# Two score banks instead of one tile of two, five W2 splits on VectorE, and a drain list in thirds of an L1 piece, in a fused attention and mixture-of-experts kernel

## The chip, the cores and the metric

The kernel runs on one core of a Trainium2 chip. The metric is the device time of one execution in microseconds (us), the median over several runs. Engines are called PE (TensorE, matmul), DVE (VectorE), ACT (ScalarE), POOL (GpSimd) and SP (SyncE, which only issues transfers here).

## The reference

Chunked attention feeds a top-1 mixture of experts:

```python
scores = scale * np.matmul(q_c, k_c.transpose(0, 1, 2, 4, 3))     # 64 x 64 within each chunk
attn = softmax(scores); x = matmul(attn, v_c)                     # as 4608 tokens x 512
do_compute = (x @ w_skip) > 0
e_idx = np.argmax(xc @ w_gate, axis=1)                            # one of 8 experts, gate_w its probability
h = np.maximum(xc[mask] @ w1[e], 0.0)                             # 512 -> 1024
y[mask] = gate_w[mask, None] * (h @ w2[e])                        # 1024 -> 512
out[do_compute] = xc + y
```

## The kernel before, in words

**Attention loop (L677 to L716).** 36 tiles of 128 tokens pass through a software pipeline: scores (PE, L240), their copy to SBUF (ACT, L245), row maximum (DVE, L250), subtraction (POOL, L255), exp (ACT, L259), transposes (PE, L266; ACT copy L271), the product with V (PE, L279), normalisation (ACT L285, DVE L290 and L292), transposes of the result (PE, L307), its split into a high and a low float16 part (ACT L312, DVE L317), and the router's logits (PE, L324). Every float32 operand that goes through the float16 matmuls is held as such a pair, high (ACT) and low (DVE).

**Routing.** For each of four groups of tiles, `route` (L374) is a generator of small steps, most of them on DVE: expert choice, ranks (PE, L402 to L406), a one-hot table (L434 to L442), and its product on PE (L446), which is added to `acc` (L450). After the last group, `tables()` (L810) walks through the rest: `order()` sorts the experts by size (L543 to L560, and the order goes to SP as `sexp`, with which the weights of the later experts are loaded), `finish_idx`, `select()` (L564 to L574, whose `sidx` the POOL gathers need), and `plan()` (L581 to L617).

**First expert, early.** Expert 3 is worked on first, and its first 256 rows ("the first unit") are gathered before the attention ends. Its W1 is converted during the loop (L357, L358). Its W2 arrives as eight pieces of 128 rows, two to a staging buffer `wst` (four buffers in all). `w2_scales` (L360) lets ACT write each piece's high part and scale the piece in place; `w2_splits` (L367) lets POOL subtract the high part to get the low one (L369). L1 of the first unit is the generator `l1_steps` (L479): eight pieces, each 12 matmuls of 128x256 into one PSUM bank, in three steps of 4 matmuls, then ACT (L490) and DVE (L491) empty the bank into `ht`.

**The drain (L719 to L764)** is a list written by hand: the last two tiles' attention steps, the router's steps, and, between them, `take(l1, n)`, `take(scales, n)` and `take(splits, n)`, which pull n steps from the three generators. Each engine then runs its own instructions in the order in which this list issued them. While the attention pools are alive, L1's pieces use the two halves of the score tile `spq` in turn (`early_hp`, L651). `spq` is one tile of two PSUM banks, and the built program makes a matmul into either half wait for the readers of the other.

**After the drain** the attention's PSUM is given back, and L1 continues in three `hp` banks. The loop over units (L845) finishes the first unit's L1, then runs L1 of the second unit (128 rows, the third early block, 128 columns to a matmul), then L2 of the first unit in two phases (`l2_split`, L515: phase 0 uses W2's high parts, phase 1 the low parts; PE lines L518), two blocks into two `sp` banks. Behind these matmuls, `take(steps, 1)` issues one step of `tables()`, and `take(splits, 1)` one split. Then comes L2 of the second unit (L511), the third unit of expert 3 (80 rows), and the other seven experts, with `conv_chunk` (ACT L223, DVE L224) converting their weights.

Of the kernel before, what the change touches and what calls it, by code (L numbers as in the profile page):

```python
# [44 lines left out]
XT_AT = 4  # L45
# [64 lines left out]
def moe_attention_kernel(ctx: ExitStack, tc: tile.TileContext, qk: bass.AP, vv: bass.AP, cst: bass.AP, crow: bass.AP, wall: bass.AP, out: bass.AP):  # L110
# [73 lines left out]
    spq = ps_p.tile([P, 2, H, CH], F32, name="spq")  # L184
# [49 lines left out]
    def pe_scores(t):  # L234
        q = T[t].pop("q").rearrange("p (c j s) -> p c j s", c=2, j=KC)
        k = T[t].pop("k").rearrange("p a (c j s) -> p c j a s", c=2, j=KC)
        sp = spq[:, t % 2]
        for j in range(KC):
            for c in range(2):
                nc.tensor.matmul(sp[halves[c], 2 * j:2 * j + 2, :], q[:, c, j, :], k[:, c, j], start=True, stop=True, skip_group_check=True)  # L240
        T[t]["sp"] = sp
# [118 lines left out]
    def w2_scales():  # L360
        for st, hi, _ in cw2:
            nc.scalar.activation(hi, st, AF.Copy, scale=SW)
            yield
            nc.scalar.activation(st, st, AF.Copy, scale=SW)
            yield

    def w2_splits():  # L367
        for st, hi, lo in cw2:
            nc.gpsimd.tensor_tensor(lo, st, hi, op=ALU.subtract)  # L369
            yield  # L370
# [280 lines left out]
    def early_hp():  # L651
        hps[0] += 1
        return spq[:, (hps[0] + 1) % 2].rearrange("p h s -> p (h s)")
# [67 lines left out]
    take(l1, 1)  # L721
# [4 lines left out]
    take(scales, 1)  # L726
# [5 lines left out]
    take(l1, 3)  # L732
    ac_exp(b)
    take(scales, 1)
    take(splits, 1)
# [7 lines left out]
    take(l1, 1)  # L743
# [5 lines left out]
    take(splits, 1)  # L749
# [5 lines left out]
    take(l1, 2)  # L755
# [3 lines left out]
    take(scales, 2)  # L759
    take(splits, 1)  # L760
    pe_logits(a)
    take(l1, 3)
# [47 lines left out]
    def tables():  # L810
        for n in (3, 0, 0, 0, 0, 2, 1, 1, 0, 1, 0, 1, 0, 1) + (0,) * 9 + (1,):
            for _ in range(n):
                route_step()
            yield
        route_step()
        yield
# [28 lines left out]
    for i, (p, bs, offs, n) in enumerate(units):  # L845
# [16 lines left out]
        for done in l1:  # L862
            at += 1
            if not i:
                take(steps, 1)
                take(scales, 2)
# [9 lines left out]
        if not i:  # L876
            for _ in l1_steps(xt, lambda: w, hc, units[1][3], hp_of[0], lambda fc: None):
                take(steps, 1)
                take(scales, 2)
            ys = [ps_s.tile([P, H, CH], F32, name="sp").rearrange("p h s -> p (h s)") for _ in bs]  # L880
            for phase in range(2):
                for y, o in zip(ys, offs):
                    for _ in l2_split(y, ht, w, o, phase):
                        take(steps, 1)
                        take(splits, 1)
                        for m in range(XGB):
                            fetch(m)
            for b, y in zip(bs, ys):
                prev.append(blk_out([(y, 0, P)], recs_b[b], xgs[b]))
# [98 lines left out]
```

## Time and profile before

| what | value |
|---|---|
| median of 3 runs | 362.99 us (361.44 to 364.69) |
| the profiled execution | 363.88 us, of which 362.1 us are the span from first to last instruction |
| mean granted PE clock | 0.966 |

| stretch, us of the span | what runs | PE busy | granted PE clock | DMA share |
|---|---|---|---|---|
| 0 to 122 | attention loop | 111.23 | 1.00 | 0.95 |
| 122 to 158 | drain, L1 of the first two units | 28.23 of 36 | 0.81 | 0.39 |
| 158 to 182 | L2 of the first two units | 19.87 of 24 | 0.86 | 0.47 |
| 182 to 192.5 | third unit | 9.58 of 10.5 | 1.00 | 0.93 |
| 192.5 to 300 | experts 2 to 6 in the sorted order | 107.12 of 107.5 | 1.00 | 0.68 |
| 300 to 362.1 | the rest | 53.62 of 62.1 | 0.96 | 0.37 |

A row of a timeline gives the start, the duration, the engine, the line, the tile that is written and those that are read, the count, and in brackets how long the engine had been idle and what ended it. A waits row gives the waiting engine and line, what it waited for, the total, the times, and the longest.

### The profile page before, as it was taken

To read this page: it belongs to the slowest core of one execution; us is meant where nothing else is said; L and a number is where in the kernel's file an instruction comes from. 1 tells how busy PE (TensorE), PEld (TensorE's weight loads), DVE (VectorE), ACT (ScalarE), POOL (GpSimd) and SP (SyncE) were. 2 spreads that over 40 slices of the span, in tenths; PEclk is the share of its full clock that TensorE was granted. 3 is DMA by queue.
4 is the path that set the end of the run, shared out by engine and by line. 5 is a ranking of instruction groups with operands and counts; after the bars stand their busy time and mean duration, and the time that the engine had idled before them with its cause. 6 is when DMAs were issued, how large, how long until landed. Compare 5 with 4: busy or idle time off the path is not lost.

```text
span 362.1 us, 10135 instructions
## 1 busy us (share of the span) xinstructions
PE 329.6 (91%) x3996; PEld 234.3 (65%) x3996; DVE 259.0 (72%) x481; ACT 192.1 (53%) x368; POOL 115.9 (32%) x116
## 2 busy tenths in 40 slices
PE   4799899999989877985989999999999999999991
PEld 1588778888878755851465544765755757668580
DVE  5368798888889933789486995785867968767430
ACT  1488887777777746510354744453643644446120
POOL 7333233333335231038260055225127322111111
PEclk9999999999999985998799999999999999999997
DMA  6999999999999990045284677876567667564000
GB/s 215 328 320 302 333 334 310 307 338 323 329 312 326 365 361 17 3 135 140 95 311 172 223 246 259 276 234 212 186 224 233 216 216 232 186 196 146 31 23 29
DMA packets 34981, 81.85 MB, mean 226 GB/s; under 512 B 4831, under 2 KB 4832, under 8 KB 34930
## 3 DMA queue, kind: packets, MB, share of 16 engines
q1 hardware_dynamic: 31826, 71.83, 60.3%
q0 software_dynamic: 3104, 9.33, 7.2%
q8 instruction: 33, 0.54, 0.6%
q14 instruction: 18, 0.15, 0.1%
HBM read 67.11 MB, written 14.17 MB: 224 GB/s over the span
## 4 chain that ended last, share of the span: by engine, by line
PE 53%; DVE 10%; issue 2%; POOL 2%; ACT 2%; POOLq 0%; DVEq 0%; ACTq 0%
PE sp L511 24%; PE hp L486 19%; PE xt L475 2%; DVE ht L491 2%; DVE ys L530 2%; PE spq L486 1%; DVE wset L224 1%; POOL wset L369 1%; PE spq L240 1%; PE sp L518 1%; PE o L279 1%; PE xp L307 1%; DVE emp L459 1%; PE pt L266 1%; POOL xg L227 1%
## 5 line engine op out<-in xcount | busy, mean ns | idle before, releaser
L486 PEld LDWEIGHTS <-wset 128*128 128x128 f16 x960 | 80.8, 100 | 30.7 <-issue 13.2
L486 PE MATMUL hp<-xt,wset 128*128 128x288 f16 (+8 forms) x912 | 94.6, 264 | 3.4 <-DVE ht L491 3.2
L511 PE MATMUL sp<-wset,ht 128*128 128x512 f16 (+7 forms) x504 | 92.3, 381 | 0.0
L224 DVE SCALAR_TENSOR_TENSOR wset<-wst,wset 128x1024 f16<-128x1024 f32 x56 | 67.6, 1217 | 8.2 <-ACT wset L223 8.0
L511 PEld LDWEIGHTS <-ht 128*128 128x128 f16 (+7 forms) x504 | 41.2, 102 | 41.7 <-issue 3.4
L223 ACT ACTIVATE wset<-wst 128x1024 f16<-128x1024 f32 x56 | 57.9, 1049 | 2.9 <-DMA wst<-in_wall 2.9
L255 POOL TENSOR_TENSOR sc<-sc,mx 128x512 f32<-128x512 f32 x36 | 37.6, 1044 | 66.7 <-DVE mx L250 66.6
L490 ACT ACTIVATE ht<-hp 128x288 f16<-128x288 f32 (+8 forms) x76 | 27.5, 362 | 59.2 <-PE hp L486 57.9
L227 POOL DMA_INDIRECT out<-ys,sidx x18 | 25.1, 1393 | 101.4 <-DVE ys L530 86.7
L491 DVE SCALAR_TENSOR_TENSOR ht<-hp,ht 128x288 f16<-128x288 f32 (+8 forms) x76 | 28.9, 392 | 19.0 <-ACT ht L490 18.2
L240 PE MATMUL spq<-k,q 128*64 128x128 f32 x576 | 39.9, 280 | 0.7 <-ACT sc L245 0.7
L476 ACT ACTIVATE xt<-xt 128x512 f16<-128x512 f32 (+7 forms) x20 | 10.3, 513 | 50.5 <-PE xt L475 50.5
L240 PEld LDWEIGHTS spq<-k,q 128*64 128x64 f32 x576 | 31.1, 137 | 7.5 <-issue 4.7
L250 DVE TENSOR_REDUCE mx<-sc 128x8 f32<-128x512 f32 x36 | 24.6, 682 | 15.1 <-ACT sc L245 14.3
L245 ACT ACTIVATE sc<-spq 128x512 f32<-128x512 f32 x36 | 21.5, 598 | 18.6 <-PE spq L240 18.6
L477 DVE SCALAR_TENSOR_TENSOR xt<-xt 128x512 f16<-128x512 f32 (+7 forms) x20 | 11.7, 586 | 25.3 <-ACT xt L476 25.1
L317 DVE SCALAR_TENSOR_TENSOR xs<-xp,xs 128x512 f16<-128x512 f32 x36 | 24.5, 681 | 5.3 <-ACT xs L312 5.2
L271 ACT ACTIVATE ps<-pt 128x512 f32<-128x512 f32 x36 | 21.5, 597 | 11.9 <-PE pt L266 11.5
L227 POOL DMA_INDIRECT xg<-out,sidx x18 | 24.9, 1385 | 8.2 <-issue 4.0
L292 DVE TENSOR_TENSOR x<-o,rr 128x512 f32<-128x512 f32 x36 | 24.9, 691 | 3.5
L279 PE MATMUL o<-v,ps 64*64 64x65 f32 x1152 | 25.4, 224 | 0.7 <-issue 0.4
L266 PE MATMUL pt<-csb,px 128*128 128x128 f32 x144 | 23.2, 284 | 2.1 <-ACT px L259 2.0
(126 smaller groups left out, 363.4 us busy)
## 6 DMA issues: line engine op xcount, KB each, us to landing
wst<-in_wall SPq DMA_DIRECT2D x56, 512.0 KB, 4.0
v<-in_vv SPq DMA_DIRECT2D x36, 260.0 KB, 4.6
q<-in_qk SPq DMA_DIRECT2D x36, 256.0 KB, 4.6
k<-in_qk SPq DMA_DIRECT2D x72, 128.0 KB, 4.5
out<-x SPq DMA_DIRECT2D x36, 256.0 KB, 4.4
wst<-in_wall SPq DMA_DIRECT2D x16, 256.0 KB, 4.9
csb<-in_cst SPq DMA_DIRECT2D x1, 348.5 KB
xg<-out,sidx POOLq DMA_INDIRECT x18, 6.1
```

Of the source, the lines that this page charges most:

```text
L223: nc.scalar.activation(w[:, 0, fc, :], st, AF.Copy, scale=SW)
L224: nc.vector.scalar_tensor_tensor(w[:, 1, fc, :], st, SW, w[:, 0, fc, :], op0=ALU.mult, op1=ALU.subtract)
L227: ins = nc.gpsimd.indirect_dma_start(**kw)
L240: nc.tensor.matmul(sp[halves[c], 2 * j:2 * j + 2, :], q[:, c, j, :], k[:, c, j], start=True, stop=True, skip_group_check=True)
L255: nc.gpsimd.tensor_tensor(sc, sc, T[t].pop("mx").unsqueeze(2).to_broadcast([P, H, CH]), op=ALU.subtract)
L266: nc.tensor.transpose(pt[:, j, :], px[:, j * P:(j + 1) * P], ident)
L279: nc.tensor.matmul(o[halves[c], a, j * VW:(j + 1) * VW], pt[halves[a], j, halves[c]], v[halves[a], c, j, :], start=True, stop=True, skip_g ...
L292: nc.vector.tensor_tensor(x.rearrange("p (j a d) -> p a j d", j=KC, a=2), o[:, :, :, :D], rr.to_broadcast([P, 2, KC, D]), op=ALU.mult)
L486: nc.tensor.matmul(hp, w()[:, a, fc, j * P:(j + 1) * P], xt[:, b, j, :n], start=(m == 0), stop=(m == 11))
L490: nc.scalar.activation(ht[:, 0, fc, :n], hp, AF.Relu)
L491: nc.vector.scalar_tensor_tensor(ht[:, 1, fc, :n], hp, 0.0, ht[:, 0, fc, :n], op0=ALU.max, op1=ALU.subtract)
L511: nc.tensor.matmul(y[c * P // cg:c * P // cg + n], ht[:, a, fc, o:o + n], w[:, b, fc, P * KC:], start=(f == 0 and m == 0), stop=(f == fw - ...
```

## The change

- `spq` becomes two tiles of one bank each. Scores and the early L1 pieces use them in turn.
- W2's pieces 3 to 7 are split by DVE instead of POOL (`scalar_tensor_tensor`, scaling in the same instruction, as `conv_w1` does), so ACT no longer scales these five in place. POOL keeps pieces 0 to 2. The five DVE splits are issued in L2 of the first unit.
- The drain takes L1 in 2, 4, 3 and 3 steps (four whole pieces) instead of 1, 3, 1, 2 and 3 (three and a third); scales and splits move in the list.
- In the loop over units: the first unit's L1 takes one scale per step instead of two, the third block's transposes stand at step 8 instead of 4, and `tables()` gets a table of 39 places instead of 25, so that `order()` starts during L2.
- The first unit's outputs (`blk_out`) are issued during its L2, block by block, not after it.

```diff
-XT_AT = 4
+XT_AT = 8
+W2_POOL = 3
...
-    spq = ps_p.tile([P, 2, H, CH], F32, name="spq")
+    spq = [ps_p.tile([P, H, CH], F32, name=f"spq{m}") for m in range(2)]
...
-        sp = spq[:, t % 2]
+        sp = spq[t % 2]
...
     def w2_scales():
-        for st, hi, _ in cw2:
+        for m, (st, hi, _) in enumerate(cw2):
             nc.scalar.activation(hi, st, AF.Copy, scale=SW)
             yield
-            nc.scalar.activation(st, st, AF.Copy, scale=SW)
-            yield
+            if m < W2_POOL:
+                nc.scalar.activation(st, st, AF.Copy, scale=SW)
+                yield
 
     def w2_splits():
-        for st, hi, lo in cw2:
-            nc.gpsimd.tensor_tensor(lo, st, hi, op=ALU.subtract)
+        for m, (st, hi, lo) in enumerate(cw2):
+            if m < W2_POOL:
+                nc.gpsimd.tensor_tensor(lo, st, hi, op=ALU.subtract)
+            else:
+                nc.vector.scalar_tensor_tensor(lo, st, SW, hi, op0=ALU.mult, op1=ALU.subtract)
             yield
...
-        return spq[:, (hps[0] + 1) % 2].rearrange("p h s -> p (h s)")
+        return spq[(hps[0] + 1) % 2].rearrange("p h s -> p (h s)")
...
-    take(l1, 1)
+    take(l1, 2)
     pe_pv(a)
     ac_rr(a)
     ve_norm(a)
     store_x(BIGQ)
-    take(scales, 1)
     pe_xtrans(a - 1)
     ac_hi(a - 1)
     ve_lo(a - 1)
     pe_logits(a - 2)
     route_step()
-    take(l1, 3)
     ac_exp(b)
     take(scales, 1)
-    take(splits, 1)
+    take(l1, 4)
     pe_ptrans(b)
...
-    take(l1, 1)
     pe_pv(b)
...
     take(scales, 2)
-    take(splits, 1)
     while len(routes) > 1 or not done_g or done_g[-1] < NG - 2:
...
-    take(l1, 2)
+    take(splits, 1)
+    take(l1, 3)
     pe_xtrans(b)
     ac_hi(b)
     ve_lo(b)
-    take(scales, 2)
-    take(splits, 1)
     pe_logits(a)
+    take(scales, 3)
+    take(splits, 2)
     take(l1, 3)
     pe_logits(b)
...
     def tables():
-        for n in (3, 0, 0, 0, 0, 2, 1, 1, 0, 1, 0, 1, 0, 1) + (0,) * 9 + (1,):
-            for _ in range(n):
+        at = {0: 3, 7: 2, 8: 1, 10: 1, 14: 1, 18: 1, 22: 1, 37: 1, 38: 1}
+        for m in range(39):
+            for _ in range(at.get(m, 0)):
                 route_step()
             yield
-        route_step()
-        yield
         yield from order()
...
-                take(scales, 2)
+                take(scales, 1)
...
             for phase in range(2):
-                for y, o in zip(ys, offs):
+                for b, y, o in zip(bs, ys, offs):
                     for _ in l2_split(y, ht, w, o, phase):
+                        out_prev()
+                        take(splits, 1)
                         take(steps, 1)
-                        take(splits, 1)
                         for m in range(XGB):
                             fetch(m)
-            for b, y in zip(bs, ys):
-                prev.append(blk_out([(y, 0, P)], recs_b[b], xgs[b]))
+                    if phase:
+                        prev.append(blk_out([(y, 0, P)], recs_b[b], xgs[b]))
+            out_prev()
```

How the order of instructions moves is shown at three places. Line numbers of the changed kernel are up to 5 higher.

**DVE in the drain**, from the last table of group 2 (`bv`) to the last group's logits (`lgs`). `ht0<-spq` are the evictions of the first unit's L1 pieces, `xs` the low parts of attention tiles, `x` the last tile's output. Before:

```order
L442 TENSOR_TENSOR bv_2682<-cl_2617,rvs_153 128x512
L491 SCALAR_TENSOR_TENSOR ht0_175<-spq_149,ht0_175 128x256
L317 SCALAR_TENSOR_TENSOR xs_2770<-xp_2765,xs_2770 128x512
L290 RECIPROCAL rr_2802<-rr_2802 128x8
L292 TENSOR_TENSOR x_2805<-o_2785,rr_2802 128x2x4x64
...
L491 SCALAR_TENSOR_TENSOR ht0_175<-spq_149,ht0_175 128x256
L317 SCALAR_TENSOR_TENSOR xs_2836<-xp_2831,xs_2836 128x512
L491 SCALAR_TENSOR_TENSOR ht0_175<-spq_149,ht0_175 128x256
L383 TENSOR_REDUCE lgs_2872<-lg_155 128x99
```

and with the change:

```order
L447 TENSOR_TENSOR bv_2683<-cl_2618,rvs_154 128x512
L496 SCALAR_TENSOR_TENSOR ht0_176<-spq0_149,ht0_176 128x256
L496 SCALAR_TENSOR_TENSOR ht0_176<-spq1_150,ht0_176 128x256
L318 SCALAR_TENSOR_TENSOR xs_2779<-xp_2774,xs_2779 128x512
L291 RECIPROCAL rr_2807<-rr_2807 128x8
L293 TENSOR_TENSOR x_2810<-o_2790,rr_2807 128x2x4x64
...
L496 SCALAR_TENSOR_TENSOR ht0_176<-spq0_149,ht0_176 128x256
L318 SCALAR_TENSOR_TENSOR xs_2845<-xp_2840,xs_2845 128x512
L496 SCALAR_TENSOR_TENSOR ht0_176<-spq1_150,ht0_176 128x256
L388 TENSOR_REDUCE lgs_2883<-lg_156 128x99
```

Four pieces are emptied ahead of `lgs` instead of three, from two tiles in turn, and the first two directly behind each other.

**DVE around the sort of the experts** (`key`, `gt` and what follows; `ht` are the evictions of the second unit's L1). Before:

```order
L491 SCALAR_TENSOR_TENSOR ht_2925<-hp_3048,ht_2925 128x128
L450 TENSOR_TENSOR acc_156<-acc_156,rk_3068 128x128
L491 SCALAR_TENSOR_TENSOR ht_2925<-hp_3063,ht_2925 128x128
L545 SCALAR_TENSOR_TENSOR key_3093<-rk_3091,rsb_97 1x8
L547 TENSOR_TENSOR c8_3095<-rk_3091,rsb_97 1x8
L550 TENSOR_TENSOR gt_3102<-key_3093 1x64
```

and with the change:

```order
L496 SCALAR_TENSOR_TENSOR ht_2971<-hp_3119,ht_2971 128x128
L374 SCALAR_TENSOR_TENSOR wset_174<-wst_2204,wset_174 128x512
L374 SCALAR_TENSOR_TENSOR wset_174<-wst_2357,wset_174 128x512 x2
L455 TENSOR_TENSOR acc_157<-acc_157,rk_3146 128x128
L374 SCALAR_TENSOR_TENSOR wset_174<-wst_2443,wset_174 128x512
L550 SCALAR_TENSOR_TENSOR key_3171<-rk_3169,rsb_97 1x8
L552 TENSOR_TENSOR c8_3173<-rk_3169,rsb_97 1x8
L374 SCALAR_TENSOR_TENSOR wset_174<-wst_2443,wset_174 128x512
L555 TENSOR_TENSOR gt_3180<-key_3171 1x64
```

All eight evictions of the second unit now stand ahead of `acc` (three did before), and the five splits stand between them and the sort. Further on, the first unit's first output `ys` stands behind `nend`, with six and more steps of `plan()` behind it; before, both outputs stood behind the whole plan.

**POOL from the last subtraction of the attention to the first outputs** (`idx` and `sidx` are gathers of rows, `out<-ys` scatters). Before:

```order
L369 TENSOR_TENSOR wset<-wst,wset 128x512 x2
L227 DMA xg<-out,idx_2812 128x512
L369 TENSOR_TENSOR wset<-wst,wset 128x512
L429 CAST rvs<-sums 128x11
L430 TENSOR_TENSOR rvs<-sums,rvs 128x11
L227 DMA xg<-out,idx_3134 80x512
L369 TENSOR_TENSOR wset<-wst,wset 128x512
L227 DMA xg<-out,sidx 128x512 x3
L227 DMA xg<-out,sidx 16x512
L369 TENSOR_TENSOR wset<-wst,wset 128x512 x4
L227 DMA out<-ys,idx_2151 4608x512
```

and with the change:

```order
L228 DMA xg<-out,idx_2816 128x512
L372 TENSOR_TENSOR wset<-wst,wset 128x512 x3
L434 CAST rvs<-sums 128x11
L435 TENSOR_TENSOR rvs<-sums,rvs 128x11
L228 DMA xg<-out,idx_3212 80x512
L228 DMA xg<-out,sidx 128x512 x3
L228 DMA xg<-out,sidx 16x512
L228 DMA out<-ys,idx_2152 4608x512
```

The four splits that stood behind the `sidx` gathers are gone from POOL, and the three that stay stand together, behind the gather of the third early block.

More of the change, by code (lines that the diff above doesn't have):

```diff
@@ L878, in moe_attention_kernel @@
                 take(steps, 1)
-                take(scales, 2)
+                take(scales, 1)
             ys = [ps_s.tile([P, H, CH], F32, name="sp").rearrange("p h s -> p (h s)") for _ in bs]
             for phase in range(2):
-                for y, o in zip(ys, offs):
+                for b, y, o in zip(bs, ys, offs):
                     for _ in l2_split(y, ht, w, o, phase):
+                        out_prev()
+                        take(splits, 1)
                         take(steps, 1)
-                        take(splits, 1)
                         for m in range(XGB):
                             fetch(m)
-            for b, y in zip(bs, ys):
-                prev.append(blk_out([(y, 0, P)], recs_b[b], xgs[b]))
+                    if phase:
+                        prev.append(blk_out([(y, 0, P)], recs_b[b], xgs[b]))
+            out_prev()
             ht, l1 = hc, ()
```

## The prediction

> **What bounds the kernel now.** I read the page first.
>
> ```profile
> span 362.1 us, 10135 instructions
> PE 329.6 (91%) x3996; PEld 234.3 (65%) x3996; DVE 259.0 (72%) x481; ACT 192.1 (53%) x368; POOL 115.9 (32%) x116
> PEclk9999999999999985998799999999999999999997
> ```
>
> PE is the bound, and the two dents in its clock show where it loses time. The windows by stage (PE busy, then the other engines, granted clock, DMA share, GB/s) say how much:
>
> ```profile
> 122.00:158.00 36.00, 28.23 (x345) 23.34 (x344) 21.47 (x62) 18.65 (x42) 7.05 (x9) 0.81 0.39 144
> 158.00:182.00 24.00, 19.87 (x97) 8.66 (x95) 18.55 (x36) 3.55 (x5) 12.52 (x12) 0.86 0.47 142
> 192.50:300.00 107.50, 107.12 (x719) 64.40 (x716) 82.80 (x107) 55.17 (x81) 34.79 (x23) 1.00 0.68 221
> ```
>
> From 192.5 us on PE is full and DMA at 0.68, so what is won before 182 should reach the end. The change touches exactly 122 to 182. PE's waits there (total, times, longest):
>
> ```profile
> PE spq L486 <- DVE ht L491: 4.9, 3, 2.7
> PE sp L518 <- POOL wset L369: 4.1, 4, 2.2
> PE hp L486 <- DVE ht L491: 1.5, 1, 1.5
> PE rk L565 <- DVE emp L458: 0.9, 1, 0.9
> ```
>
> With 0.3 us behind `ps` that is 11.7 us of waiting. The rest is the clock. Cut into stretches of 3.41 us, the trace shows it granted either whole or at half:
>
> ```profile
> 125.53:128.95 3.42, 2.26 (x31) 2.18 (x31) 1.11 (x3) 2.21 (x5) 1.17 (x1) 1.00 1.03 386
> 128.95:132.36 3.41, 1.48 (x39) 1.00 (x38) 2.73 (x6) 1.91 (x5) 0.97 (x1) 1.00 1.01 379
> 132.36:135.77 3.41, 2.63 (x20) 2.18 (x20) 0.79 (x4) 0.73 (x2) 1.22 (x2) 0.50 0.91 323
> ...
> 142.60:146.01 3.41, 3.41 (x18) 2.61 (x17) 0.00 (x0) 3.32 (x7) 0.00 (x0) 0.50 0.02 5
> 146.01:149.42 3.41, 3.41 (x41) 3.10 (x40) 3.11 (x10) 1.95 (x5) 0.43 (x2) 1.00 0.02 5
> ...
> 166.50:169.91 3.41, 0.75 (x2) 0.19 (x2) 3.41 (x3) 0.00 (x0) 3.39 (x4) 1.00 0.29 83
> 169.91:173.32 3.41, 2.42 (x6) 0.82 (x6) 3.31 (x6) 0.00 (x0) 1.52 (x2) 0.50 0.75 208
> ```
>
> A stretch with 1.48 or 0.75 us of matmul was followed by half rate, one with 2.26 was not; half rate ended only after a wholly busy stretch, 2.63 not being enough. So the waits cost twice: PE ran at half for 13.6 us in the drain and 6.8 us in L2.
>
> The timeline shows the pieces by which I price:
>
> ```profile
> 122.13 0.60 PE L486 MATMUL spq<-xt,wset 128*128 128x256 f16 x4
> 126.22 0.42 DVE L491 SCALAR_TENSOR_TENSOR ht<-spq,ht 128x256 f16<-128x256 f32 x1
> 126.69 0.60 PE L486 MATMUL spq<-xt,wset 128*128 128x256 f16 x4 [1.30 <-DVE ht L491]
> ...
> 133.13 1.01 PE L486 MATMUL spq<-xt,wset 128*128 128x256 f16 x4 [2.71 <-DVE ht L491]
> ...
> 142.30 1.86 PE L486 MATMUL hp<-xt,wset 128*128 128x256 f16 x8 [1.52 <-DVE ht L491]
> ...
> 158.09 7.93 PE L518 MATMUL sp<-wset,ht 128*128 128x512 f16 x36
> 168.17 0.38 PE L518 MATMUL sp<-wset,ht 128*128 128x512 f16 x1 [2.15 <-POOL wset L369]
> ...
> 181.46 2.12 PE L486 MATMUL hp<-xt,wset 128*128 128x80 f16 x48
> ```
>
> At full rate 36 matmuls of 512 columns take 7.93 us, 0.22 each; by columns that is 0.11 at 256 and 0.055 at 128.
>
> **The change part by part.** PE's work from 122.13 to 181.46 stays the same: the first unit's L1 96 x 0.11 = 10.6, the second's 96 x 0.055 = 5.3, L2 of both 72 x 0.22 = 15.8, and, at about the same price by columns, the attention's last matmuls 4.3 and routing with transposes 2.2. Sum 38.2 us, against 59.3 elapsed: 11.7 listed waits, and 9.4 of half rate and small gaps. The question is which waits the new order keeps.
>
> *Two score tiles and a retimed drain.* The wait at 126.69 ends with the DVE eviction at 126.22 of piece 0, although piece 1 goes to the other bank. With two tiles a piece waits only for the piece two before it, and by the order on DVE that one has long been emptied. The three spq waits (4.9 us) and what followed them at half rate go. Walking the new order from 122.13: PE is at the second attention product at 123.04 as before (eight matmuls fit where four and 0.3 us of idling stood), ends piece 1 at 126.1, piece 2 at 129.5, piece 3 at 131.8, with 0.4 us of waiting for the last tile's `x`.
>
> What is late next is the first `hp` piece. It takes the bank that `lgs` reads, so it waits for `lgs`, and on DVE `lgs` stands behind the eviction of piece 3, which on ACT stands behind three W2 scales. Rows:
>
> ```profile
> 139.10 0.36 DVE L383 TENSOR_REDUCE lgs<-lg 128x99 f32<-128x198 f32 x1 [1.30 <-PE lg L324]
> 140.83 0.26 DVE L399 TENSOR_TENSOR eh<-csb,vals 128x99 f16<-128x99 f32 x1
> L364 ACT ACTIVATE wst<-wst 128x512 f32<-128x512 f32 x8 | 5.0, 628 | 0.2
> ```
>
> ACT's last `xs` would end at 131.1, three scales at 0.63 at 132.7 (they overlap by 0.1 each), ACT's eviction 133.0, DVE's 133.4, `lgs` 133.7. PE stands from 132.1: a wait of 1.7 us. `hp` starts at 133.8 instead of 142.3.
>
> The rank table needs `eh`, 2.0 us behind `lgs`. Here the three POOL splits get in the way, back to back behind the gather of the third block (131.0), some 132 to 135.5:
>
> ```profile
> 165.15 0.45 DVE L602 TENSOR_TENSOR bv<-bv,nb 1x288 f32<-1x288 f32 x1
> 166.79 4.96 DVE L609 TENSOR_TENSOR bv<-bv,cap 1x288 f32<-1x288 f32 x1
> 166.96 4.48 POOL L369 TENSOR_TENSOR wset<-wst,wset 128x512 f16<-128x512 f32 x4
> ```
>
> A DVE operation that takes 0.45 us took 4.96 until POOL's four splits were over. So I let `eh` end at 136.8, not at 135.7; PE reaches the rank matmuls at 137.2 either way and does not wait. But DVE is then late: its table steps and the evictions of the second unit share one queue, and L1 of that unit needs only 0.65 us per piece. I book 2.6 us of waits there (below: none, as in the old order, where the same evictions left PE no listed wait before 153; above: 4, twice the table's two long steps). L2 starts at 147.8 instead of 158.1.
>
> *Splits.* The 4.1 us of waiting for POOL and half rate behind it (6.8 us at half) go if DVE is in time:
>
> ```profile
> L358 DVE SCALAR_TENSOR_TENSOR wset<-wst,wset 128x512 f16<-128x512 f32 x8 | 5.5, 690 | 2.9 <-ACT wset L357 2.9
> 154.65 0.14 DVE L545 SCALAR_TENSOR_TENSOR key<-rk,rsb 1x8 f32<-1x8 f32 x1
> 155.95 0.17 DVE L560 CAST oh<-oh 1x64 f16<-1x64 f32 x1
> 157.23 1.86 DVE L463 TENSOR_TENSOR fin<-acc 128x32 f32<-128x32 f32 x1
> 163.94 0.14 DVE L596 CAST nend<-cs 1x1 int32<-1x1 f32 x1
> ```
>
> The same instruction in the loop took 0.69 us, so five take 3.5. They start behind the last eviction (148.5) and end at 152.9; PE needs the first low part after 32 matmuls, at 155.4. Covered by 2.5 us; were the cover gone, each missing split would cost PE at most 0.7 us. ACT drops five scales, 3.1 us, off the path.
>
> *What waits instead.* The sort (`gt` to `oh` 1.3 us) then ends at 154.2, and PE's selection matmul at 155.5 finds it ready. From there to `nend` DVE took 7.8 us, of which 1.7 is the `fin` operation held up by POOL, so 6.1 now: 160.3. Behind it stands the first output `ys`, 0.7 us, and the second unit's L2 needs its `sp` bank. PE ends the first unit's L2 at 159.0 and waits for 161.0: 2.0 us that were not there before (below: none, if the plan's steps run shorter; above: 3.5).
>
> *Weights of the next expert.* `sexp` comes at 154.1 instead of 156.0, and the staging buffers are all free by 152.9 (before, the last at 171.4). The first conversions, at some 163, find the first loads landed (512 KB in 4.0 us). The outputs issued earlier and the gathers moved ahead on POOL cost nothing: PE needs the first `sidx` gather at 168.6, issued at 158.3.
>
> *Sum.* Work 38.2, waits 0.4 + 1.7 + 2.6 + 2.0 = 6.7: 44.9 instead of 59.3, 14.4 us less. The profiled execution took 363.88 us (1.8 outside the span), so 349.5; the median of the runs shown lies 0.9 lower. I forecast 349.0, in its own range 345 to 353: the terms without the new waits give 342, and small gaps and the upper ends 353.
>
> *Clock.* The longest new wait is 2.0 us. The Trainium skill ("TensorE: Matmul & The Clock Gate", section "HAM oscillation — how this bites in real kernels") says to avoid PE idle gaps of over some 3.4 us. By that rule no new wait slows the clock, and the sum stays. The trace here is harsher: the longest gap ahead of the drop at 132.36 was 2.71 us.
>
> **The rivals.**
> 1. *The clock drops again.* For it: a stretch holding most of the 2.0 us wait, or the scattered waits of the second unit's L1, would have 1.4 to 2 us of matmul in 3.41, and the trace dropped at 1.48. Against: it held at 2.26, and L2 runs 10 us without a wait. Half rate for two stretches costs up to 3.4 us, in L1 and in L2 once each some 5: 354.
> 2. *The drain's waits only move.* ACT and DVE evict as slowly as before, so L1 gains nothing and only L2's 4.1 us and its half rate (2.9 us of 5.8 busy) go: 356.9. Against: the waits end with the wrong bank's eviction.
> 3. *The weights set the pace*, so the end moves only with `sexp`: 1.9 us, 362. For it: ACT waited for `wst` loads after 210. Against: PE stayed full there, DMA at 0.68.
> 4. *Slower: PE never leaves half rate between the `hp` wait (132) and L2's end.* Place: pieces of 0.65 us waiting for DVE's queue, then late splits. It decides if no 3.41 us stretch is wholly busy. Price: 48 x 0.11 + 96 x 0.055 + 48 x 0.22 = 21 us more, less 6 us of waits that vanish in it: 364 to 366. Against: L2's first 32 matmuls wait for nothing.
>
> **How the numbers follow.** Forecast 0.60, clock 0.17, drain only moves 0.11, weights 0.07, slower 0.05. This kernel's measurement tells about 1% (3.6 us) from no change. Faster by over 1%: 0.60 + 0.17 + 0.11 = 0.88; within 1%: 0.07; slower 0.05. The range 345 to 357.5 holds the first three.
>
> **What would show it.** Right: the spq and POOL rows gone from PE's waits, `hp` starting near 134, L2 near 148, the third unit near 167 instead of 181.5, PE's clock at 1.00 through the drain, one new wait of about 2 us of the second unit's L2 for `ys`, full PE behind. Wrong: PE waiting for `wset` written by DVE, a half-rate stretch in L2, or a third unit that starts early with PE idle after 192.

## The result, and the profile after

The changed kernel takes 351.75 us (median of four executions, 349.94 to 353.65), the kernel before 363.84 (now four executions too, 361.44 to 366.62): a ratio of 0.967 with a 95% interval of 0.958 to 0.976. A second measurement gave 352.12 and 0.964 (0.959 to 0.969). The forecast was 349.0, in a range of 345 to 357.5: the sign and the range hold, the median lies 2.7 us above the forecast. The profiled execution of the changed kernel is its fastest, 349.94 us. A ratio leaves out executions that took over 1.5% more than the fastest of their kernel; a median has them in.

The page of the changed kernel:

```profile
span 348.1 us, 10133 instructions
PE 321.3 (92%) x3996; PEld 231.0 (66%) x3996; DVE 255.0 (73%) x486; ACT 188.4 (54%) x363; POOL 112.7 (32%) x111
PEclk9999999999999999999999999999999999999997
```

PE's clock has no dent left ahead of the last slice, which read 7 before too. PE is busy for 8.3 us less than before although it does the same matmuls: what is missing is matmul time at half rate. PE's waits from 122 to 185 us in the changed kernel (total, times, longest):

```profile
PE hp L491 <- DVE ht L496: 2.5, 4, 1.4
PE hp L491 <- DVE lgs L388: 1.7, 1, 1.7
PE sp L516 <- DVE cs L599: 1.6, 1, 1.6
```

The rows `spq` and POOL's `wset` are gone, and PE waits for no `wset` that VectorE writes. Two of the three rows that stand there now were booked: `lgs` at 1.7 and, at 2.0, the second unit's L2 (here at 1.6; the row names `cs`, an operation of the plan that stands ahead of `ys` on DVE). The first row has four waits, of which one of 0.7 belongs to the second unit's L1, where I had booked 2.6. The other three are in the third unit, where I had expected what stood there before. PE's timeline after the change has the milestones:

```profile
122.51 1.04 PE L491 MATMUL spq<-xt,wset 128*128 128x256 f16 x8
124.80 1.91 PE L491 MATMUL spq<-xt,wset 128*128 128x256 f16 x16
...
134.39 3.67 PE L491 MATMUL hp<-xt,wset 128*128 128x256 f16 x32 [1.69 <-DVE lgs L388]
...
143.17 4.33 PE L491 MATMUL hp<-xt,wset 128*128 128x128 f16 x72 [0.69 <-DVE ht L496]
147.34 1.89 PE L523 MATMUL sp<-wset,ht 128*128 128x512 f16 x8
...
160.56 1.46 PE L516 MATMUL sp<-wset,ht 128*128 128x512 f16 x6 [1.60 <-DVE cs L599]
...
166.02 1.71 PE L491 MATMUL hp<-xt,wset 128*128 128x80 f16 x36
169.10 0.59 PE L491 MATMUL hp<-xt,wset 128*128 128x80 f16 x12 [1.37 <-DVE ht L496]
...
178.23 16.41 PE L491 MATMUL hp<-xt,wset 128*128 128x400 f16 x96
```

`hp` starts at 134.39 (forecast 133.8), L2 at 147.34 (147.8), the third unit at 166.02 (166.7; before 181.46). The 16 matmuls at 124.80 run through from one L1 piece into the next. The windows of the changed kernel (PE busy, PEld, DVE, ACT, POOL, clock, DMA share, GB/s), the first the whole stretch from the first L1 matmul to the third unit, the last most of what follows:

```profile
122.51:166.02 43.51, 39.33 (x422) 28.11 (x419) 34.99 (x100) 18.51 (x42) 13.35 (x14) 1.00 0.50 182
190.00:300.00 110.00, 108.97 (x775) 68.19 (x774) 84.78 (x112) 54.92 (x84) 38.11 (x25) 1.00 0.70 227
```

The stretch takes 43.51 us where it took 59.33, with 39.33 of matmul and 4.18 without. Behind 190 us PE is full with DMA at 0.70: the weights did not become the pace.

**Where the 12 us are.** Between the two profiled executions the stretch gives 15.8 us. The part behind it, from the third unit to the span's end, takes 182.1 us instead of 180.6, so 1.5 are given back there (0.6 against the 181.5 of the second profile of before, below), and the loop ahead of it ended 0.4 later. That makes 13.9, the difference of the two times (363.88 and 349.94).

### The profile page after: what moved, and what is told of

The parts are those of the page before. It is cut to its first block, busy times and chain, and to the rows that moved or that the text cites. A ratio compares the mean times of both kernels' runs of the same rounds, so it can differ in the third digit from the quotient of the medians.

```text
span 348.1 us, 10133 instructions
## 1 busy us (share of the span) xinstructions
PE 321.3 (92%) x3996; PEld 231.0 (66%) x3996; DVE 255.0 (73%) x486; ACT 188.4 (54%) x363; POOL 112.7 (32%) x111
## 4 chain that ended last, share of the span: by engine, by line
PE 48%; DVE 9%; ACT 2%; issue 2%; POOLq 0%; DVEq 0%; ACTq 0%
PE sp L516 24%; PE hp L491 21%; PE xt L480 2%; DVE wset L225 2%; DVE ys L535 1%; DVE ht L496 1%; PE sp L523 1%; ACT wset L363 1%; ACT ht L495 0%; DVE ex L393 0%; DVE xt L482 0%; POOLq L987 0%; ACT wst L366 0%; DVE ys L575 0%; ACT wset L224 0%
## 5 line engine op out<-in xcount | busy, mean ns | idle before, releaser
L491 PE MATMUL hp<-xt,wset 128*128 128x288 f16 (+8 forms) x912 | 93.1, 262 | 5.5 <-DVE ht L496 3.6
L491 PEld LDWEIGHTS <-wset 128*128 128x128 f16 x960 | 79.3, 98 | 24.9 <-issue 6.9
L228 POOL DMA_INDIRECT xg<-out,sidx x18 | 26.8, 1488 | 7.5 <-issue 4.3
L280 PEld LDWEIGHTS o<-v,ps 64*64 64x64 f32 x1152 | 20.3, 133 | 7.4 <-issue 6.9
```

The lines of the kernel that those rows point to most:

```text
L228: ins = nc.gpsimd.indirect_dma_start(**kw)
L280: nc.tensor.matmul(o[halves[c], a, j * VW:(j + 1) * VW], pt[halves[a], j, halves[c]], v[halves[a], c, j, :], start=True, stop=True, skip_g ...
L491: nc.tensor.matmul(hp, w()[:, a, fc, j * P:(j + 1) * P], xt[:, b, j, :n], start=(m == 0), stop=(m == 11))
```

## The experiments

The median of a few executions tells 1% at best here, and the profiles say why: the loop ahead of the change ended anywhere between 122.1 and 128.4 us, with the same instructions in it. Two profiles of the kernel before and two of the changed one also show how far a reading repeats. So I read each kernel by the **stretch**, from PE's first L1 matmul to the third unit's first, and by the rest behind it. All kernels in one table; "list" is the retimed drain together with the retimed loop over units (every move of the change but the other two parts), "tiles" the two score tiles, "splits" the five splits on VectorE, and the ratio is to the kernel before, run on the same chip.

| kernel | L1 starts | third unit | stretch | rest | median us | ratio (95%) |
|---|---|---|---|---|---|---|
| before | 122.13 | 181.46 | 59.3 | 180.6 | 363.84 | |
| before, second profile | 122.90 | 179.32 | 56.4 | 181.5 | 362.56 (one) | |
| tiles | 124.27 | 178.28 | 54.0 | 180.6 | 360.97 | 0.986 (0.977-0.995) |
| splits | 125.10 | 180.44 | 55.3 | 180.7 | 361.76 | 0.992 (0.987-0.996) |
| tiles, splits | 128.43 | 177.70 | 49.3 | 181.4 | 354.97 | 0.970 (0.966-0.975) |
| list | 124.40 | 173.81 | 49.4 | 182.1 | 360.96 | 0.990 (0.986-0.994) |
| list, splits | 125.06 | 170.58 | 45.5 | 181.8 | 353.41 | 0.972 (0.964-0.981) |
| list, tiles | 124.66 | 172.01 | 47.4 | 182.0 | 356.18 | 0.979 (0.973-0.984) |
| all three (the change) | 122.51 | 166.02 | 43.5 | 182.1 | 351.75 | 0.967 (0.958-0.976) |
| the change, second profile | 123.90 | 167.38 | 43.5 | 182.1 | 352.12 | 0.964 (0.959-0.969) |
| before, idle matmuls added | 124.20 | 180.74 | 56.5 | 180.7 | 363.05 | 0.997 (0.992-1.002) |
| change, plan late | 126.39 | 168.14 | 41.8 | 180.6 | 349.80 | 0.962 (0.953-0.970) |
| change, `lgs` first | 122.33 | 164.73 | 42.4 | 181.8 | 352.47 | 0.971 (0.964-0.979) |
| change, both of these | 125.30 | 165.96 | 40.7 | 180.5 | 346.83 | 0.953 (0.945-0.960) |

For "tiles, splits" the five executions took 354.0, 354.9, 355.0, 360.0 and 360.9 us. The profile shows the longest, with two dips of the clock in its loop; the ratio rests on the three near 355.

**1. The two tiles alone.** My theory: the wait is for the wrong bank's eviction, so the tiles free PE, and the list follows.

```diff
-    spq = ps_p.tile([P, 2, H, CH], F32, name="spq")
+    spq = [ps_p.tile([P, H, CH], F32, name=f"spq{m}") for m in range(2)]
...
-        sp = spq[:, t % 2]
+        sp = spq[t % 2]
...
-        return spq[:, (hps[0] + 1) % 2].rearrange("p h s -> p (h s)")
+        return spq[(hps[0] + 1) % 2].rearrange("p h s -> p (h s)")
```

> The kernel before with the score banks as two tiles and nothing else. Theory (the wait was for the wrong bank's eviction, and it cost twice, by waiting and by the half clock behind it): the 4.9 us of spq waits fall under 1, the drain's clock stays at 1.00, and with a new wait of 1 to 2 us of the first hp piece the kernel gains 7 to 10 us, 354 to 357 where the kernel before takes 364; L2 still waits 3 to 4 us for POOL's wset. Rival (the retimed list is what frees PE): at least 3 us of waiting stay in the drain, at another row, the clock drops again, and the gain is under 3 us.

The `spq` waits fell to 0.2 us, as expected: the wait was for the wrong bank's eviction. But 361.0 us is far from 354 to 357, and the timelines of PE and ACT in this kernel say where waiting stayed:

```profile
139.11 1.45 PE L486 MATMUL hp<-xt,wset 128*128 128x256 f16 x8 [2.75 <-DVE ht L491]
```

```profile
136.87 0.28 ACT L393 ACTIVATE lh<-ex 128x88 f32<-128x88 f32 x1 [1.47 <-DVE ex L388]
137.06 0.61 ACT L362 ACTIVATE wset<-wst 128x512 f16<-128x512 f32 x1
137.70 0.63 ACT L364 ACTIVATE wst<-wst 128x512 f32<-128x512 f32 x1
138.24 0.37 ACT L490 ACTIVATE ht<-spq 128x256 f16<-128x256 f32 x1
```

The first `hp` piece waits 2.75 us, because the old list issues the last drain piece's eviction behind the routing's `lh` and two scales on ACT. In the first profile of before it waited 1.52 us, but in the second (experiment 6) it already waited 2.35:

```profile
141.54 1.03 PE L486 MATMUL hp<-xt,wset 128*128 128x256 f16 x8 [2.35 <-DVE ht L491]
```

So little of the `spq` waits moved to this place. PE reaches the `hp` pieces 14.8 us behind the first L1 matmul, where before took 20.2 and 18.6: the tiles alone shorten the drain by 3.8 to 5.3 us. The whole stretch is 2.4 to 5.3 us shorter, by which profile of before one takes. The clock dropped in the drain too, for one stretch of 3.4 us. The rival was right in that waiting stays at another row and the clock drops again; its price, a gain under 3 us, is not decided (the interval of the ratio is 2 to 8 us).

**2. The list with one tile.**

```diff
-    spq = [ps_p.tile([P, H, CH], F32, name=f"spq{m}") for m in range(2)]
+    spq = ps_p.tile([P, 2, H, CH], F32, name="spq")
...
-        sp = spq[t % 2]
+        sp = spq[:, t % 2]
...
-        return spq[(hps[0] + 1) % 2].rearrange("p h s -> p (h s)")
+        return spq[:, (hps[0] + 1) % 2].rearrange("p h s -> p (h s)")
```

> The changed kernel with the score banks as one tile again, its list and the five splits on VectorE kept. Theory: each L1 piece waits for the eviction of the piece before it again, but the list puts a step of the attention between most pieces, so only the second piece, which follows the first without a break, waits: a row spq of 1.3 to 2 us, no half clock (over 1.7 us of matmul in 3.41), 1 to 3 us slower than the changed kernel. Rival A (the two tiles are what counts): over 4 us of spq waits, half clock behind them, 8 us or more slower. Rival B (the list alone does it): within 1 us.

One row of PE's timeline carries the difference to the changed kernel, whose 16 matmuls ran through here:

```profile
129.76 1.47 PE L491 MATMUL spq<-xt,wset 128*128 128x256 f16 x12 [1.81 <-DVE ht L496]
```

A wait of 1.81 us at the second piece, no half clock, a stretch 2.0 us longer, the median 1.7 higher. So with the list in place the tiles are worth 2 us, no more.

**3. The five splits alone**, with ScalarE's second scale of these pieces dropped, as in the change.

```diff
+W2_POOL = 3
...
-            nc.gpsimd.tensor_tensor(lo, st, hi, op=ALU.subtract)
+            if m < W2_POOL:
+                nc.gpsimd.tensor_tensor(lo, st, hi, op=ALU.subtract)
+            else:
+                nc.vector.scalar_tensor_tensor(lo, st, SW, hi, op0=ALU.mult, op1=ALU.subtract)
```

> The kernel before with the last five splits of W2 on VectorE (and ScalarE's five second scales dropped), the drain and the tiles as they were. Theory: the 4.1 us of PE's waits for POOL's wset in L2 go, and the half clock behind them (6.8 us at half, 2.9 us lost) goes with them: 356 to 358, 6 to 8 us faster than before, with the drain's waits and half clock untouched. Rival A (the splits on DVE come too late, or hold up the sort behind them): PE waits for wset written by DVE or for oh, and under 3 us are won. Rival B (only the wait counts, the clock is even): 4 us.

361.8 us, a miss: Rival A. PE waits 2.5 us in L2, now for VectorE, and 3.4 us of half clock stay there. DVE's timeline in this kernel has the five splits behind the plan's last row:

```profile
168.26 0.17 DVE L622 CAST oexp<-es 1x36 int32<-1x36 f32 x1
168.34 3.08 DVE L374 SCALAR_TENSOR_TENSOR wset<-wst,wset 128x512 f16<-128x512 f32 x5
```

PE had waited since 167.5 for the first of them. In the old list the sort and the plan are issued early and stand ahead of the splits on DVE. In the changed list they come later, and DVE splits before it sorts:

```profile
148.06 1.88 DVE L374 SCALAR_TENSOR_TENSOR wset<-wst,wset 128x512 f16<-128x512 f32 x3
150.10 0.68 DVE L374 SCALAR_TENSOR_TENSOR wset<-wst,wset 128x512 f16<-128x512 f32 x1
151.90 0.67 DVE L374 SCALAR_TENSOR_TENSOR wset<-wst,wset 128x512 f16<-128x512 f32 x1
```

The cover of 2.5 us in the prediction is thus a gift of the list and not of the moved splits: the same instructions in another place of DVE's queue are late.

**4. The changed kernel with all splits on POOL** (and ScalarE's five scales back).

```diff
-W2_POOL = 3
+W2_POOL = 8
```

> The changed kernel with all eight splits on POOL and all of ScalarE's second scales back. In this order POOL's five splits stand ahead of the gathers, not behind them as before. Theory (POOL's back-to-back operations hold up DVE's operations with two inputs from SBUF): POOL runs them at 143 to 149, PE finds them ready in L2, but DVE's table steps and the evictions behind them stall, and PE waits 2 to 5 us in the second unit's L1: 2 to 6 us slower than the changed kernel. Rival A (a split on POOL is late whatever the order): 4 us of waits for wset in L2 and half clock, 7 us slower. Rival B (only POOL's order mattered, DVE has the time): within 1 us.

The stretch is 3.8 us longer, the median 4.4 higher, and PE finds every split ready. POOL's and DVE's timelines of this kernel:

```profile
146.68 7.19 POOL L372 TENSOR_TENSOR wset<-wst,wset 128x512 f16<-128x512 f32 x5
```

```profile
148.34 1.57 DVE L447 TENSOR_TENSOR bv<-cl,rvs 128x640 f16<-128x640 f16 x1
149.84 0.28 DVE L496 SCALAR_TENSOR_TENSOR ht<-hp,ht 128x128 f16<-128x128 f32 x1
150.04 1.71 DVE L447 TENSOR_TENSOR bv<-cl,rvs 128x768 f16<-128x768 f16 x1
```

In the run with `lgs` first, where POOL was idle at that point, the same two `bv` operations took 0.82 and 0.95. PE's listed waits for evictions from 122 to 185 us grew from 2.5 to 4.9 us (within the stretch, from 0.7 to 2.8). Not all of the 3.8 us is POOL: PE also waited 1.0 us at the second unit's first piece for ACT's eviction of `xt` and 0.4 for DVE's behind it, and ACT had the returned scales ahead of it. How much each makes was not separated.

**5. Idle matmuls in the waits of the kernel before.** The prediction counted the waits twice, by the half clock behind them (9.4 us with small gaps). This run keeps the waits and takes the half clock away.

```diff
+    def pe_fill(n):
+        f = ps_t.tile([P, DM], F32, name="rk")
+        for _ in range(n):
+            nc.tensor.matmul(f, ones, zeros, start=True, stop=True)
...
-    take(l1, 2)
+    take(l1, 1)
+    pe_fill(8)
+    take(l1, 1)
...
+                        if phase and y is ys[0] and k == 1:
+                            pe_fill(8)
```

> The kernel before with sixteen idle matmuls added (ones by zeros into the rank bank, nobody reads them): eight in the 2.7 us that PE waits in the drain ahead of the third L1 piece, eight in the 2.2 us that it waits in L2 for POOL's fifth split. 3.5 us of work more, no wait removed. Theory (the waits cost twice, the second time by the half clock that follows them): PE stays at clock 1.00 from 122 to 182, and the kernel is 5 to 9 us faster than before, at 355 to 359, though it does more. Rival (the half clock fell on time that PE had anyway, the next wait took it up): within 2 us of before, or slower by the added work.

A miss: 0.997 of before. The clock stayed whole through the drain (one half stretch was left, in L2), and the stretch lost 2.8 us against the first profile of before, 5 to 9 expected; against the second (56.4, experiment 6) it lost nothing. PE's waits in the stretch of this kernel, the added matmuls' own row among them:

```profile
PE hp L491 <- DVE ht L496: 3.5, 4, 2.4
PE spq L491 <- DVE ht L496: 2.8, 2, 1.5
PE sp L523 <- POOL wset L374: 2.6, 4, 0.7
PE rk L178 <- DVE acc L455: 1.0, 1, 1.0
```

A faster PE only reaches the next eviction earlier: the `hp` row is 3.5 us, where the stretch of the first profile of before had a single `hp` wait of 1.52. Its first wait is 2.35 us, as in the second profile of before, whose clock was whole up to the same piece. The rival ("the next wait took it up") is right for most of it.

**6. The kernel before once more.**

> The kernel before, unchanged, profiled a second time. The loop ahead of the change ended between 122.1 and 126.4 us in the nine profiles so far, with the same code up to there. If this scatter is one of executions, the loop's end lies in that range again, anywhere in it, while the stretch from the first L1 matmul to the third unit's first is 59.3 within 0.5. If the stretch scatters too, the gains by stretch cannot be read to better than that.

The stretch did scatter: 56.4 instead of 59.3. The windows of the whole stretch, of the first profile of before and then of the second, show it is the clock:

```profile
122.13:181.46 59.33, 47.43 (x421) 31.34 (x419) 39.41 (x96) 22.07 (x47) 19.15 (x19) 0.83 0.42 142
```

```profile
122.90:179.32 56.42, 42.91 (x421) 29.39 (x419) 39.28 (x96) 21.77 (x47) 19.11 (x19) 0.94 0.43 149
```

Half clock for 20.5 us in the one, for 6.8 in the other, in the same program with the same 2.71 us wait. PE is busy 4.5 us less and idles 1.6 more (13.5 against 11.9): 2.9 us is what 13.6 us of half clock were worth. In stretches of 3.41 us, laid back from the drop, the second execution reads:

```profile
129.03:132.44 3.41, 2.16 (x52) 1.64 (x51) 2.05 (x6) 2.29 (x6) 0.29 (x1) 1.00 1.04 393
132.44:135.85 3.41, 1.95 (x24) 1.80 (x24) 1.62 (x4) 0.88 (x2) 1.90 (x2) 1.00 0.83 294
135.85:139.26 3.41, 1.83 (x22) 1.36 (x20) 1.71 (x5) 1.14 (x3) 1.14 (x1) 1.00 0.19 65
139.26:142.67 3.41, 1.12 (x11) 1.04 (x11) 1.37 (x6) 3.30 (x7) 0.00 (x0) 1.00 0.01 2
142.67:146.08 3.41, 3.41 (x27) 2.78 (x25) 0.80 (x2) 3.29 (x8) 0.00 (x0) 0.50 0.03 7
```

Here the 2.71 us wait (131.2 to 133.9) falls across two stretches, both keep some 2 us of matmul, and the clock holds; in the first execution (130.4 to 133.1) 1.9 us of it lay in one, ahead of the drop at 132.36. The profile from which I argued was one of two cases.

**7. The list alone, and the other two without it.** These complete the eight combinations.

```diff
-    spq = [ps_p.tile([P, H, CH], F32, name=f"spq{m}") for m in range(2)]
+    spq = ps_p.tile([P, 2, H, CH], F32, name="spq")
...
-W2_POOL = 3
+W2_POOL = 8
```

> The retimed list alone: the changed kernel with one tile for the score banks and all eight splits on POOL (ScalarE's second scales back). Measured from the first L1 matmul behind the attention loop to the third unit's first, before took 59.3 us, the changed kernel 43.5, without the two tiles 45.5, with the splits on POOL 47.4. New theory (the list carries most of the gain, the other two parts add about 2 and 4 us to it): 49 to 50 us in this stretch, 9 to 10 less than before, PE waiting some 2 us for spq and as in the run with the splits on POOL some 5 us for evictions. Rival, my first one (the two tiles free PE, the list follows): without the tiles the spq waits come back whole and the stretch takes 54 us or more.

The second is the kernel before with the edits of 1 and 3 together.

> The other two parts without the list: the kernel before with two tiles and the five splits on VectorE. New theory: the single gains of the same stretch add up, 5.3 for the tiles and 4.0 for the splits, 50 us instead of 59.3; the first hp piece still waits 2.5 to 3 us for the last L1 piece's eviction, which ACT reaches only behind lh and two scales, since the old list issues it behind the routing step; PE still waits about 2.5 us for wset written by DVE. Rival (they overlap, as the waits of one part hide in those of the other): 52 us or more.

By the stretch both hold, 49.4 and 49.3 us. The windows of the list alone and then of tiles with splits:

```profile
124.40:173.81 49.41, 40.15 (x422) 28.17 (x420) 34.44 (x95) 21.37 (x47) 20.52 (x19) 1.00 0.44 158
```

```profile
128.43:177.70 49.27, 41.78 (x421) 28.29 (x419) 36.23 (x101) 18.67 (x42) 13.38 (x14) 0.97 0.45 152
```

In each pair of rows of the table that differ in the list alone, it takes 5.8 (tiles and splits there), 9.8 (splits there), 6.7 (tiles there) or 9.9 us (neither there; 7.0 by the second profile of before); the splits take 3.8 or 3.9 with the list and 4.7 beside the tiles without it; the tiles 2.0 or 2.1 with the list, 6.1 beside the splits without it. Each row without the list but before has one profile, and before scattered by 2.9 us, so the differences to these rows are no more exact than that. No stretch of a kernel with the list has any half clock. The medians do not follow in one place: the list alone measured 0.990, tiles with splits 0.970, where stretch and rest together make them equal within 1 us. With loops that end up to 6 us apart and four or five executions each (357.7 to 362.8 us for the list, 354.0 to 360.9 for tiles with splits), this is not settled.

The timelines of the same profiles, cut at the first `hp` piece and at L2's first matmul, show where each part acts. In the drain the tiles alone save 3.8 to 5.3 us, the list alone 4.7 to 6.2 and both together 6.8 to 8.3: each does in part what the other does. With the list, the splits save their 3.8 us between the first `hp` piece and L2 (16.8 us with all splits on POOL, 12.95 without), and L2 of the first two units takes 18.7 us whichever engine splits; without the list they save 1.5 to 2.9 us in L2 itself (20.7 us instead of 22.2 to 23.5). Which of the list's own moves does how much was not separated.

**8. What the change left on the table.** First the plan, whose result is read only at the program's end:

```diff
+        while unit[0] < 3:
+            yield
         yield from plan()
```

> The changed kernel with the steps of the plan (the list for rows beyond the capacities, read only at the program's end) held back until the fourth unit. Theory: the wait of the second unit's L2 for its bank (1.6 us) goes, since the first ys stands right behind sidx at 157.4, and the third unit's wait (1.4 us and two small ones) goes too, since the conversions of the next weights stand on DVE some 5 us earlier: 2.5 to 3.5 us faster than the changed kernel, fourth unit at 175 instead of 178.2. Rival A (the plan only stood in front, PE waits for DVE's conversions anyway): only the 1.6 goes. Rival B (the end is set by the weights' loads): PE's waits grow behind 180 by what is won, within 1 us.

The L2 wait for `ys` is gone, the third unit's waits fell from 1.85 to 0.94 us, and the fourth unit starts 52.8 us behind the first L1 matmul instead of 55.7: 2.9 us, as the theory had it. The absolute 175 was missed, since this loop ended 3.9 us later. The medians (349.8 and 351.8) do not separate the two kernels: their intervals overlap. DVE's timeline of this kernel, ahead of the third unit:

```profile
164.92 0.49 DVE L482 SCALAR_TENSOR_TENSOR xt<-xt 128x320 f16<-128x320 f32 x1 [1.29 <-ACT xt L481]
165.86 3.50 DVE L225 SCALAR_TENSOR_TENSOR wset<-wst,wset 128x1024 f16<-128x1024 f32 x3 [0.45 <-ACT wset L224]
```

DVE now idles and the three conversions wait for ACT's halves, so 0.8 us of the third unit's wait stays. Then the eviction ahead of `lgs`:

```diff
-    take(scales, 3)
-    take(splits, 2)
     take(l1, 3)
     pe_logits(b)
     route_step()
+    take(scales, 3)
+    take(splits, 2)
```

> The changed kernel with the drain's last three scales and two POOL splits moved behind the routing step that issues lgs. Theory: the first hp piece's wait (1.7 us) for lgs comes from piece 3's eviction standing behind the three scales on ACT; it falls to 0.3 or less, hp starts near 132.8 instead of 134.4, and 1 to 2 us reach the end. Rival (the time is only handed on: POOL's splits then run under the table's steps, eh and the second unit's evictions are held up): PE waits the 1.5 us at the rank matmuls or in the second unit's L1, within 0.7 us of the changed kernel.

The `hp` wait fell from 1.69 to 1.02 us, not to 0.3, and the stretch by 1.1. PE's and DVE's timelines of this kernel show the floor:

```profile
132.17 0.35 PE L325 MATMUL lg<-wsg,xs 128*128 128x18 f16 x8
133.54 3.67 PE L491 MATMUL hp<-xt,wset 128*128 128x256 f16 x32 [1.02 <-DVE lgs L388]
```

```profile
132.79 0.42 DVE L496 SCALAR_TENSOR_TENSOR ht<-spq,ht 128x256 f16<-128x256 f32 x1 [0.61 <-ACT ht L495]
133.13 0.35 DVE L388 TENSOR_REDUCE lgs<-lg 128x99 f32<-128x198 f32 x1
```

The scales were only 0.7 us of it. The rest is the piece's own chain: ACT's eviction, DVE's, then `lgs`. The medians cannot tell this run from the changed kernel (352.5 and 351.8).

> Both of these edits. Theory: their gains add up, 3.5 to 5.5 us faster than the changed kernel, near 347. Rival: what lgs wins is eaten by DVE later, no better than the plan held back alone.

Both together: 346.83 us, 0.953 (0.945 to 0.960), a stretch of 40.7 and a rest of 180.5. From L1's first matmul to the fourth unit it takes 51.7 us, 4.0 less than the change: 2.9 and 1.1, so the gains add up. It is the fastest of all kernels here, some 5 us below the changed one; the two intervals only just touch.

> The changed kernel again, on the chip of the other three. By the stretch it should take 43.5 within 0.5, and the median 351.8 within 1.5; the loop's end may lie anywhere between 122 and 126.5.

The last run repeats the changed kernel: 43.5 us again, equal to 0.03 us, while its loop ended 1.4 later. As far as two profiles show, the change makes the stretch not only shorter but steady.

## Why the prediction was right, and where it was not

**Right: the walk of the new order.** The times of the new order were not got by subtracting waits from the old one, but by following PE, ACT and DVE through the new list. For the profiled execution this gave 349.5; it took 349.94. The waits for `lgs` (1.7, measured 1.69) and for `ys` (2.0, measured 1.6) came where they were booked. `eh` was done at 136.96 (136.8) and the splits at 152.6 (152.9), and PE waited for neither of these two.

**Right by two errors that cancel.** The stretch was forecast at 44.9 us and took 43.5: the new waits are 4.2 us (43.51 less 39.33) and not 6.7, the matmul work is 39.3 and not 38.2. The mis-sized term is the 2.6 us for the second unit's L1, which was 0.7. Against this stands a term that I left out. I took what follows the third unit as it was. DVE's timeline of the changed kernel shows the plan's steps and then the first conversions of the next weights on DVE just when the third unit starts:

```profile
164.86 0.24 DVE L622 CAST oexp<-es 1x36 int32<-1x36 f32 x1
165.02 0.47 DVE L482 SCALAR_TENSOR_TENSOR xt<-xt 128x320 f16<-128x320 f32 x1
165.42 3.47 DVE L225 SCALAR_TENSOR_TENSOR wset<-wst,wset 128x1024 f16<-128x1024 f32 x3
168.82 0.22 DVE L496 SCALAR_TENSOR_TENSOR ht<-hp,ht 128x80 f16<-128x80 f32 x1
```

The third unit's `ht` evictions stand behind 3.5 us of conversions, PE waits 1.37 us and more, and the rest grows to 182.1. With the plan held back the waits halve and the rest is 180.6 again: shown. That the total came out within 0.5 us is partly luck, and the profile of before has a part in it: by its second profile the stretch shrank by 12.9 us, by its first by 15.8, and 14.4 were forecast. I had asked of this place whether the loads would have landed by then (they had), and not what stands behind the conversions.

**Wrong: what the change's parts are worth.** "The three spq waits (4.9 us) and what followed them at half rate go" was priced under one heading with the retimed drain, but the reason given was the two tiles. They do take the `spq` waits away, and alone they shorten the drain by 3.8 to 5.3 us; but the list alone shortens it as much or more, and with the list in place the tiles are worth 2 us. "five take 3.5 [...] Covered by 2.5 us" was put down to the place of the splits behind the last eviction; in the old list they stand behind the plan and PE waits 2.5 us for them. The retimed list carries the most, 6 to 10 us. The sum came out since the walk used the new list throughout. Rival 2 (the drain's waits only move, and L1 gains nothing) does not hold for the tiles alone either: 2.75 us of waiting stay at the first `hp` piece, but the drain is shorter.

**Wrong: the price of half clock.** "So the waits cost twice" holds at less than half the price: 13.6 us of half clock, 6.8 if nothing else were in the way, cost 2.9. Where PE waits for evictions, it can be slow at no cost until the next eviction is done. Nor did the drop at 132.36 follow a gap of 2.71 us: only 1.9 us of that gap lay ahead of it. Summed from the first profile, 11.7 of waits and 9.4 of half rate and gaps, it looked as if the whole were there to be won; in the second profile PE idles longer at a higher rate.

**The 2.7 us of the median** do not show in the stretch or in the rest: both repeat within 0.1 us in the second profile of the change, and the 1.4 us by which that execution was longer are all in the loop ahead of it. The two profiled loops of before ended at 122.1 and 122.9, the changed kernel's at 122.5 and 123.9, those of other kernels with the same loop at up to 128.4. The sum was made against one execution with an early end. That the loop of the changed kernel is later on average was not tested; its instructions are the same, apart from the bank's tile.

Of the prediction's rivals, the clock did not drop again: no half clock in the stretch in either profile of the change, although a stretch of 3.41 us there can hold as little as 1.72 us of matmul, the rest being the 1.69 us wait:

```profile
132.23:135.64 3.41, 1.72 (x23) 1.48 (x21) 2.06 (x5) 1.34 (x3) 3.39 (x4) 1.00 0.78 275
```

The weights did not set the pace (PE busy for 108.97 of 110 us behind 190), and the slower case did not come, since PE ran at full rate through the whole stretch.

## What to carry to other kernels

Price a list of issues by walking it in full: the same split buffer was worth 2 us or 6, and the same five splits were in time or late, by what stood ahead in an engine's queue. Part of a wait that vanishes comes back at the next wait in line, two cures of one wait do not add up, and more than half of the slow clock's price was hidden in waits here; so none of these is to be added up as a gain. Where executions scatter by more than the question, read a stretch between two landmarks of the trace instead of the median, and look at more than one profile of the kernel before.

## What the runs showed of the hardware

- **The clock's drop depends on where a wait falls, not on its length alone.** The same 2.71 us wait was followed by half rate in one execution and not in the other. In the two profiles of before, stretches of 3.41 us with 1.12 and 1.48 us of matmul were followed by half rate, stretches with 1.83, 1.95 and 2.16 were not. Matmul time alone is not the rule: in other runs, laid from their own drops in the same way, a stretch with 1.40 us was not followed by half rate (141.11 to 144.52, tiles with splits), and one with 1.83 was (108.91 to 112.32, in the loop of the run with the plan late). The windows to lay are those that fit the drop itself. Half rate ended behind a stretch with 2.85 us of matmul (169.97 to 173.38, second profile of before), not only behind a wholly busy one as the prediction read it; behind 2.72 it went on (166.87 to 170.28, tiles alone). All half-rate times were multiples of 3.4 us (3.4, 6.8, 10.2, 13.6, 20.5). The Trainium skill's advice ("TensorE: Matmul & The Clock Gate", "HAM oscillation — how this bites in real kernels") to avoid idle gaps of over some 3.4 us did not suffice here: half rate also came with gaps of 2.71 and 2.35 us.
- **The drops of one execution lie whole stretches apart, and their place differs between executions.** With tiles and splits the clock dropped at 42.12, 113.80 and 168.42 us, 21 and 16 times 3.413 apart. Counted in such stretches from the span's start, that is 1.2 us into a stretch; with the splits alone it is 0.6, in the first profile of before 2.6. The Trainium skill ("TensorE: Matmul & The Clock Gate", "Part 1: The HAM clock gate") says that the window runs freely and does not start with the kernel. These executions agree. In the two profiles of before the places happen to agree within 0.1 us (drops at 132.34 and 142.66, three stretches apart); what differs is that the second loop ended 0.77 us later, and the wait with it.
- **A group of POOL operations and DVE's operations with two SBUF inputs slow each other both ways.** Five POOL splits took 7.19 us beside DVE's `bv` products (1.44 each), four took 4.48 (1.12 each) in the kernel before; the two products took 1.57 and 1.71 us instead of 0.82 and 0.95. The evictions between them, which read PSUM and SBUF, took 0.28 us in both cases.
